# Causal mask: from TensorE matmuls to the VectorE instruction that finds the row maximum

## The chip, the cores and the metric

One core of a Trainium2 chip runs the whole program in one launch. The metric is the device time of the program in microseconds, the median of several runs. Five engines matter: TensorE (matmuls and transposes, results in PSUM), VectorE and ScalarE (element work, both can read and write PSUM), GpSimd (element work in SBUF) and the SP queue, which issues the DMAs. In the profile they are PE (PEld is its weight load), DVE, ACT, POOL and SP. [...]

## The reference

Causal attention with an additive bias over 4 batches, 8 heads, 576 tokens and a head dimension of 64, then two feed-forward blocks over the 2304 tokens:

```python
scores = scale * np.matmul(q, k.transpose(0, 1, 3, 2))
causal = np.triu(np.ones((S, S), dtype=bool), k=1)
cum = np.cumsum(np.maximum(s, 0.0), axis=-1)
bias = -(cum[:, :, :, None] - cum[:, :, None, :])
scores = np.where(causal, -1000000000.0, scores + np.minimum(bias, 0.0))
scores = scores - np.max(scores, axis=-1, keepdims=True)
attn = np.exp(scores)
attn = attn / (np.sum(attn, axis=-1, keepdims=True) + 1e-09)
out = np.matmul(attn, v)

x = out.transpose(0, 2, 1, 3).reshape(B * S, H * D)     # 2304 x 512
x = ((x @ w_a) * (x @ w_b)) @ w_out                     # 512 -> 1536 -> 512
r = np.maximum(x @ w_in, 0.0)                           # 512 -> 2048
out = (r * r) @ w_out2
```

The change concerns the line with `np.where` and the one with `np.max`.

## The kernel before, in words

Three kinds of work follow one another and overlap. Attention works head by head, 32 heads in all. A head's 576 queries are five row blocks (`kb`, L383): one of 64 rows and four of 128. The scores of a head fill four PSUM banks (`banks`, L462): blocks 1 and 2 with 192 and 320 keys, blocks 0 and 3 with 64 and 448 keys, then block 4 in two halves of 288 keys each. A row block needs only the keys up to its last row, so just the piece that holds its last m columns, the diagonal piece, has anything to mask: five of the six pieces of a head.

`softmax` (L555) fills a bank with score matmuls (`st`), whose bias comes in through two extra rows of the operands. The first batch uses one float32 matmul a piece, the later ones two matmuls of split operands (`T` and `t2k`, `t2q`). Before the change the mask is added by TensorE as well: for each diagonal piece one more matmul accumulates `mask` times `identb`, a 128 x 128 bfloat16 tile of -1e9 above the diagonal times an identity (L587 to L592). VectorE then takes each piece's row maximum, negated, into `neg` (L608). Block 4 has two halves, so the smaller of two such values is taken once more (L615). ScalarE writes exp(score + neg) to `e` and the row sums to `sum` (L621). VectorE turns the sums into reciprocals `one`, and VectorE, ScalarE or GpSimd scales `e` by them (L632 to L643). `weigh` (L646) transposes the weights on TensorE into PSUM (`pt`), copies them to SBUF (`ph`, and a low part `pl` in later batches) and multiplies them with the values (`av`).

The first feed-forward block (`moe1`, L834) uses its own matmuls (`ab`, `py`) in chunks of up to 512 tokens, and its weights are decoded on VectorE, ScalarE and GpSimd (`roomxh`, `roomxl`, `words`) while attention runs. The second block (`ph` of hidden units, `po`) comes last.

The order of all this isn't the order of the code. Every operation is given to a planner (`Plan.order`, L145) with a cost in nanoseconds for each engine that may do it, and the planner plays the program through: on each engine the ready operation of the best rank starts next, and some copies and scalings go to whichever engine is free first. On TensorE attention ranks ahead of the feed-forward block, so that `ab` and `py` matmuls fill the places where attention has to wait. The plan fixes each engine's order. The first batch has nothing to fill it with, since the feed-forward block needs its result. In the plan a mask matmul costs 56 (L592) and a row maximum 150 + 1.04 n (L325). Every instruction of the program is issued from L246, so the profile's rows differ by tile names and not by lines. `st`, `neg`, `e`, `one`, `pt`, `ph`, `pl`, `av`, `u`, `vl` belong to attention.

## Time and profile before

| | |
|---|---|
| median of 3 runs | 1128.77 us (1125.85 to 1129.11) |
| span of the profiled execution | 1128.5 us |
| instructions | 15440 |
| TensorE busy over the span | 97% |
| VectorE busy | 55% |
| ScalarE busy | 43% |
| GpSimd busy | 28% |

The profiled execution is one of its own; its span lies 0.3 us under the median. Busy shares over the whole span mix three stages, so the rows below are taken by stretches. [...] What a matmul costs is read from the starts: how much later the next one begins. [...]

### The profile page before, as it was taken

Reading aid. Unit: us, or ns where it says so; the run is one execution under the profiler, and the core shown is the slowest. Engines: PE = TensorE matmul, PEld = TensorE weight load, DVE = VectorE, ACT = ScalarE, POOL = GpSimd, SP = SyncE. Lnnn points to the kernel's source line nnn. Section 1 sums busy time; section 2 is a strip of 40 time slices with the busy share of each in tenths; the row PEclk is TensorE's granted clock in tenths of the full one; section 3 lists DMA queues with packets and bytes.
Section 4 is the critical chain, followed back from the end, with each engine's and each line's share of the span. In section 5 each row is a group of like instructions: output and inputs, shape, how many; then the busy total and the mean of one; then the engine's idle time right before and its main releaser. Section 6 shows DMA issues by size and latency. Waiting matters only on the chain.

```text
span 1128.5 us, 15440 instructions
## 1 busy us (share of the span) xinstructions
PE 1099.6 (97%) x5488; PEld 928.5 (82%) x5488; DVE 625.6 (55%) x1174; ACT 482.9 (43%) x1121; POOL 318.4 (28%) x274
## 2 busy tenths in 40 slices
PE   5998999999999999999999999999999999999998
PEld 3665777778899999899999999888888888888887
DVE  5776797878777777723222358987232232232232
ACT  4545686667666665421121244445232222232222
POOL 2434655655433333200100147766010010000000
PEclk9977899999999999999999999999999999999999
DMA  6433467666544443443433677642110010010010
GB/s 206 153 110 105 142 194 229 187 207 194 151 148 130 135 143 103 143 147 116 164 108 116 186 246 234 195 147 75 38 38 1 21 54 1 1 57 1 1 38 19
DMA packets 83692, 132.10 MB, mean 117 GB/s; under 512 B 9104, under 2 KB 53648, under 8 KB 83616
## 3 DMA queue, kind: packets, MB, share of 16 engines
q1 hardware_dynamic: 83616, 131.12, 37.1%
q8 instruction: 43, 0.70, 0.3%
q14 instruction: 33, 0.27, 0.1%
HBM read 99.54 MB, written 22.69 MB: 108 GB/s over the span
## 4 chain that ended last, share of the span: by engine, by line
PE 90%; DVE 6%; DMA 2%; issue 1%; SPq 0%; ACT 0%; POOL 0%; DVEq 0%; ACTq 0%; POOLq 0%
PE ab L246 24%; PE ph L246 17%; PE po L246 17%; PE py L246 12%; PE av L246 7%; PE st L246 7%; PE pt L246 5%; DVE e L246 1%; DMA roomxh<-in_moe_w_a 1%; SPq L246 0%; DVE neg L246 0%; DMA v_0r<-in_moe_w_in 0%; DVE v_1t L246 0%; DMA v_1r<-in_moe_w_out 0%; DVE v_0t L246 0%
## 5 line engine op out<-in xcount | busy, mean ns | idle before, releaser
L246 DVE SCALAR_TENSOR_TENSOR ph<-ph,r 128x512 f32<-128x512 f32 (+1 forms) x80 | 51.6, 645 | 195.0 <-ACT r L246 195.0
L246 ACT ACTIVATE r<-ph 128x512 f32<-128x512 f32 (+1 forms) x80 | 44.5, 556 | 212.5 <-PE ph L246 212.5
L246 PE MATMUL po<-w2h,g2h 128*128 128x512 f32 x288 | 112.4, 390 | 0.0
L246 PE MATMUL po<-w2h,g2l 128*128 128x512 f32 x288 | 112.3, 390 | 0.0
L246 PE MATMUL po<-w2l,g2h 128*128 128x512 f32 x288 | 112.3, 390 | 0.0
L246 ACT ACTIVATE e<-st,neg 128x192 f32<-128x192 f32 (+2 forms) x192 | 91.1, 479 | 46.8 <-DVE neg L246 42.9
L246 PE MATMUL ab<-xh,wh 128*128 128x448 f32 x288 | 106.3, 369 | 0.0
L246 PE MATMUL ab<-xh,lo 128*128 128x448 f32 x288 | 105.3, 365 | 0.0
L246 PE MATMUL ab<-xl,wh 128*128 128x448 f32 x288 | 105.2, 365 | 0.0
L246 DVE TENSOR_TENSOR ab<-ab,a 128x448 f32<-128x448 f32 (+1 forms) x60 | 38.6, 644 | 105.1 <-PE ab L246 102.5
L246 PE MATMUL pt<-ident,e 128*128 128x128 f32 (+2 forms) x480 | 86.0, 290 | 10.9 <-DVE e L246 9.0
L246 DVE TENSOR_REDUCE neg<-st 128x1 f32<-128x192 f32 (+2 forms) x192 | 77.6, 425 | 27.9 <-PE st L246 19.8
L246 PE MATMUL py<-gh,wh 128*128 128x448 f32 (+1 forms) x240 | 90.8, 379 | 0.5 <-DVE gl L246 0.5
L246 PE MATMUL py<-gh,loo 128*128 128x448 f32 (+1 forms) x240 | 89.0, 371 | 0.0
L246 PE MATMUL py<-gl,wh 128*128 128x448 f32 (+1 forms) x240 | 88.9, 370 | 0.0
L246 PEld LDWEIGHTS pt<-ident,e 128*128 128x128 f32 (+2 forms) x480 | 55.7, 138 | 37.2 <-issue 11.7
L246 PE MATMUL av<-ph,val 128*128 128x256 f32 (+3 forms) x256 | 81.5, 409 | 3.1 <-DVE ph L246 1.4
L246 DVE TENSOR_TENSOR g2l<-ph,g2h 128x512 fp32r<-128x512 f32 (+1 forms) x80 | 51.0, 637 | 41.8 <-ACT g2h L246 37.2
L246 ACT COPY a<-ab 128x448 f32<-128x448 f32 (+1 forms) x60 | 32.6, 544 | 91.6 <-PE ab L246 91.5
L246 PE MATMUL ph<-yhy,w2h 128*128 128x512 f32 (+1 forms) x192 | 67.9, 354 | 0.4 <-DVE gl L246 0.4
L246 PE MATMUL ph<-yhy,w2l 128*128 128x512 f32 (+1 forms) x192 | 67.9, 354 | 0.0
L246 PE MATMUL ph<-yly,w2h 128*128 128x512 f32 (+1 forms) x192 | 67.9, 354 | 0.0
(205 smaller groups left out, 2640.2 us busy)
## 6 DMA issues: line engine op xcount, KB each, us to landing
lo<-wlab SPq DMA_DIRECT2D x48, 512.0 KB
loo<-wlo SPq DMA_DIRECT2D x40, 384.0 KB
v_0r<-in_moe_w_in SPq DMA_DIRECT2D x16, 512.0 KB
v_1r<-in_moe_w_out SPq DMA_DIRECT2D x16, 512.0 KB
roomxh<-in_moe_w_a SPq DMA_DIRECT2D x10, 512.0 KB
roomxh<-in_moe_w_b SPq DMA_DIRECT2D x10, 512.0 KB
roomxl<-in_moe_w_out SPq DMA_DIRECT2D x9, 512.0 KB
out<-o SPq DMA_DIRECT2D x18, 256.0 KB
```

The source lines that it names most:

```text
L246: getattr(eng, method)(*map(real, args), **{k: real(a) for k, a in kw.items()})
```

## The change

The mask becomes one 128 x 448 bfloat16 tile: 320 columns of zero, then the 128 x 128 triangle, now laid out by rows of queries. The mask matmuls and the identity in bfloat16 go. For a diagonal piece the row maximum is taken by `tensor_tensor_reduce`: it adds the last `kn` columns that end at the block's edge of the mask tile, scales by -1, writes the negated masked scores back to the same place in PSUM and keeps the row's minimum in `neg`. The exponential of such a piece then reads negated scores and undoes that by its scale of -1. The one piece without a diagonal (block 4, keys 0 to 287) keeps its reduction. In the planner's eyes the new instruction costs as much as the old one, and the 56 for each mask are gone. The tile in which the mask is made borrows another buffer, and the scratch space of the DMA descriptors is made smaller.

```diff
--- before.py
+++ after.py
@@ -425,16 +425,15 @@
         "affine_select", 128, ident, ident, pattern=[[1, P]], base=0, channel_multiplier=-1,
         compare_op=ALU.not_equal, fill=1.0,
     )
-    identb = const([P, P], BF16, "identb")
-    act("copy", 128, identb, ident)
-    maskf = at([P, 320], F32, "vl", 1, "maskf")[:, :P]
-    gps("memset", 128, maskf, 0.0)
+    MW = 320 + P
+    maskf = at([P, S], F32, "e2", 2, "maskf")[:, :MW]
+    gps("memset", MW, maskf, 0.0)
     gps(
-        "affine_select", 128, maskf, maskf, pattern=[[1, P]], base=0, channel_multiplier=-1,
+        "affine_select", P, maskf[:, 320:], maskf[:, 320:], pattern=[[-1, P]], base=0, channel_multiplier=1,
         compare_op=ALU.is_ge, fill=NEG,
     )
-    mask = const([P, P], BF16, "mask")
-    act("copy", 128, mask, maskf)
+    mask = const([P, MW], BF16, "mask")
+    act("copy", MW, mask, maskf)
 
     spos = at([P, S], F32, "raw", 2, "spos")[: B * H]
     dve("tensor_scalar_max", S, spos, ssb, 0.0)
@@ -567,7 +566,7 @@
                 wide_e = max(kb[blk][0] + kb[blk][1] for blk, _, _ in pieces) > 512
                 e = at([P, S if wide_e else 512], F32, *(("e2", 2) if wide_e else ("e1", 3)), f"e{nm}_{i}")
             off = 0
-            calls, masks, cost, got = [], [], 0, []
+            calls, cost, got = [], 0, []
             for blk, k0, kn in pieces:
                 at_, m = kb[blk]
                 qc = slice(at_, at_ + m)
@@ -582,30 +581,30 @@
                     t1, t2q, t2k, _ = head
                     both = ((t1[:66, 0, qc], t1[:66, 1, ks]), (t2q[:, qc], t2k[:, ks]))
                     cost += 2 * (max(kn, 256) / 2.4 + 13)
-                mine = [("matmul", (to, *ab), {}) for ab in both]
+                mine = [("matmul", (to, *ab), {"stop": True}) for ab in both]
                 calls = mine + calls if kn > 256 else calls + mine
-                if diag:
-                    d0 = off + at_ - k0
-                    masks.append(
-                        ("matmul", (ps[:m, d0 : d0 + m], mask[:, :m], identb[:, :m]), {})
-                    )
-                    cost += 56
                 if k0 == 0:
                     place[blk] = (e, off)
-                got.append((blk, k0, m, to, kn, e[:m, place[blk][1] + k0 : place[blk][1] + k0 + kn]))
+                got.append((blk, k0, m, to, kn, diag, e[:m, place[blk][1] + k0 : place[blk][1] + k0 + kn]))
                 off += kn
             if b == 0:
                 ins = [tq.part("x"), tq.part("c"), tk.part("x"), tk.part("c")]
             else:
                 ins = [t1, t2q, t2k]
-            calls += masks
 
             for z, (_, _, kw) in enumerate(calls):
-                kw.update(start=z == 0, stop=z == len(calls) - 1)
-            pe(cost, calls, ps, [*ins, mask, identb])
-            for blk, k0, m, to, kn, _ in got:
+                kw.update(start=z == 0, skip_group_check=z > 0)
+            pe(cost, calls, ps, ins)
+            for blk, k0, m, to, kn, diag, _ in got:
                 c = blk if k0 == 0 else nq
-                dve("tensor_reduce", kn, out=neg[:m, c : c + 1].part(c), in_=to, op=ALU.max, axis=AX.X, negate=True)
+                if not diag:
+                    dve("tensor_reduce", kn, out=neg[:m, c : c + 1].part(c), in_=to, op=ALU.max, axis=AX.X, negate=True)
+                    continue
+                edge = 320 + m
+                dve(
+                    "tensor_tensor_reduce", kn, out=to, in0=to, in1=mask[:m, edge - kn : edge], op0=ALU.add,
+                    op1=ALU.min, scale=-1.0, scalar=3.0e38, accum_out=neg[:m, c : c + 1].part(c),
+                )
             held += got
             if i + 1 < len(banks) and banks[i + 1][0][1]:
                 continue
@@ -615,11 +614,11 @@
                     op=ALU.min, axis=AX.X, reads=[neg.part(nq - 1), neg.part(nq)],
                 )
             halves = bool(pieces[0][1])
-            for blk, k0, m, to, kn, ee in held:
+            for blk, k0, m, to, kn, diag, ee in held:
                 c = blk if k0 == 0 else nq
                 n_ = nq + 1 if halves else blk
                 act(
-                    "activation", kn + 360, ee.part((blk, k0)), to, AF.Exp, bias=neg[:m, n_ : n_ + 1].part(n_),
+                    "activation", kn + 360, ee.part((blk, k0)), to, AF.Exp, bias=neg[:m, n_ : n_ + 1].part(n_), scale=-1.0 if diag else 1.0,
                     accum_out=tot[:m, blk, int(c == nq) : int(c == nq) + 1].part(c), psum=True,
                 )
             held = []
@@ -1064,7 +1063,7 @@
     import concourse.bacc as bacc
     from concourse.bass_utils import run_bass_kernel_spmd
 
-    nc = bacc.Bacc("TRN2", target_bir_lowering=False, num_devices=1)
+    nc = bacc.Bacc("TRN2", target_bir_lowering=False, num_devices=1, dynamic_dma_scratch_size=1024)
     arrays, args = {}, []
     for name in _INS:
         a = inputs[name]
```

One VectorE call becomes two instructions in the program: the main one and one that writes the accumulated value to `neg`. In the order of instructions both are named ISA.

VectorE at the very first banks of the program, before: the row maxima of the first head's first two banks (`st_0_0_0`, `st_0_0_1`) come one behind the other, and only the first of a bank waits for TensorE.

```order
L246 TENSOR_REDUCE neg_110<-st_0_0_0_135 128x1 [waits PE_49,Pool_49]
L246 TENSOR_REDUCE neg_110<-st_0_0_0_135 128x1
L246 TENSOR_REDUCE neg_110<-st_0_0_1_156 64x1 [waits PE_49]
L246 TENSOR_REDUCE neg_110<-st_0_0_1_156 128x1
L246 TENSOR_REDUCE neg_118<-st_0_1_0_169 128x1 [waits PE_49,Pool_49]
```

The same place now:

```order
L246 ISA st_0_0_0_124,neg_115<-st_0_0_0_124,mask 128x192 [waits PE_49,Pool_49]
L246 ISA neg_115 128x1
L246 ISA st_0_0_0_124,neg_115<-st_0_0_0_124,mask 128x320 [waits DVE_49]
L246 ISA neg_115 128x1
L246 ISA st_0_0_1_141,neg_115<-st_0_0_1_141,mask 64x64 [waits PE_49]
L246 ISA neg_115 64x1
L246 ISA st_0_0_1_141,neg_115<-st_0_0_1_141,mask 128x448 [waits DVE_49]
L246 ISA neg_115 128x1
```

Four instructions have become eight, and the second main one of a bank waits for VectorE itself, since it writes the same bank as the first.

TensorE at the second bank of the last head (`st_3_1_1`, blocks 0 and 3), before: two mask matmuls with their weight loads stand between the scores and the next work.

```order
L246 MATMUL st_3_1_1_5067<-T_1037 128x448
L246 MATMUL st_3_1_1_5067<-t2k_3_1_4866,t2q_3_1_4864 128x448
L246 MATMUL st_3_1_1_5067<-T_1037 64x64
L246 MATMUL st_3_1_1_5067<-t2k_3_1_4866,t2q_3_1_4864 64x64
L246 LDWEIGHTS mask
L246 MATMUL st_3_1_1_5067<-identb,mask 64x64
L246 LDWEIGHTS mask
L246 MATMUL st_3_1_1_5067<-identb,mask 128x128
L246 MATMUL av_2_1_320_5044<-ph_2_1_320_1_5029,vs_2_1_4760 128x128
```

The same place now:

```order
L246 MATMUL st_3_1_1_5085<-T_912 128x448
L246 MATMUL st_3_1_1_5085<-t2k_3_1_4839,t2q_3_1_4859 128x448
L246 MATMUL st_3_1_1_5085<-T_912 64x64
L246 MATMUL st_3_1_1_5085<-t2k_3_1_4839,t2q_3_1_4859 64x64
L246 MATMUL ab_2_1_5097<-xh_4765,wh_1_747 128x448
L246 MATMUL ab_2_1_5097<-xl_4668,wh_1_747 128x448
```

The masks are gone, a score matmul of 64 columns stands last, and the plan has moved: a filling `ab` comes behind the bank instead of an `av`, and it belongs to another chunk and another block of weights. Counted over the whole order, 708 `ab` and 324 `py` matmuls stand ahead of the last `av` now, and 672 and 288 stood there before.

## Rows read from the trace of the kernel before

**Rows 1.** By stretches: us; busy us (count) per engine, clock, DMA share, GB/s.

```profile
8.00:113.00 105.00, 93.11 (x371) 60.30 (x372) 73.14 (x167) 54.02 (x157) 39.14 (x32) 0.85 0.46 145
...
141.00:282.00 141.00, 139.76 (x741) 111.21 (x740) 121.40 (x238) 102.41 (x255) 81.89 (x61) 1.00 0.65 202
282.00:480.00 198.00, 196.99 (x1203) 177.62 (x1203) 149.57 (x341) 119.90 (x322) 65.69 (x58) 1.00 0.45 136
```

**Rows 2.** Tile `mask`: count, ns min/median/max, first and last start in us.

```profile
L246 PE MATMUL st<-identb,mask x160: 194/229/330, 9.7 to 459.6; 128*128 128x128 bf16 x128, 128*64 128x64 bf16 x32
```

**Rows 3.** Waits of TensorE, 113 to 480 us: total us, times, longest.

```profile
PE st L246 <- ACT e L246: 2.0, 2, 1.7
...
PE pt L246 <- DVE pl L246: 0.3, 1, 0.3
```

**Rows 4.** Waits of TensorE, 8 to 113 us.

```profile
PE pt L246 <- DVE e L246: 9.0, 4, 4.0
PE st L246 <- DMA fk<-cum: 7.8, 1, 7.8
```

**Rows 5.** Chain of waits, 8 to 141 us, shares by engine and tile.

```profile
by line: PE st L246 29.1%; PE av L246 26.5%; PE pt L246 16.3%; PE ab L246 7.7%; DVE e L246 7.6%; DVE neg L246 1.8%; DVE roomxl L246 1.8%; DVE u L246 1.7%; issue 1.7%; DVE ph L246 1.3%; DVE raw_1q L246 0.9%; DVE T L246 0.8%; ACT e L246 0.7%;
```

**Rows 6.** Timeline of TensorE, 410 to 440 us: start, us, operation.

```profile
412.23 0.38 PE L246 MATMUL st<-identb,mask 128*64 128x64 bf16 x2
412.41 0.45 PE L246 MATMUL ab<-xh,wh 128*128 128x448 f32 x1
412.70 0.37 PE L246 MATMUL ab<-xl,wh 128*128 128x448 f32 x1
412.91 0.37 PE L246 MATMUL ab<-xh,lo 128*128 128x448 f32 x1
...
419.47 0.28 PE L246 MATMUL av<-ph,vs 128*128 128x256 f32 x1
419.59 0.28 PE L246 MATMUL av<-pl,vs 128*128 128x256 f32 x1
...
419.98 0.23 PE L246 MATMUL st<-identb,mask 128*128 128x128 bf16 x1
420.02 0.36 PE L246 MATMUL av<-ph,vs 128*128 128x256 f32 x1
420.22 0.28 PE L246 MATMUL av<-pl,vs 128*128 128x256 f32 x1
...
424.86 0.29 PE L246 MATMUL st<-identb,mask 128*128 128x128 bf16 x2
424.95 0.45 PE L246 MATMUL st<-T 66*128 66x448 f32 x1
425.24 0.36 PE L246 MATMUL st<-t2k,t2q 128*128 128x448 f32 x1
```

**Rows 7.** Timeline of all engines, 0 to 20 us.

```profile
9.66 0.42 PE L246 MATMUL st<-identb,mask 128*128 128x128 bf16 x2
...
9.88 2.22 PE L246 MATMUL st<-fk,fq 65*128 65x448 f32 x4
```

**Rows 8.** VectorE groups by shape, whole span: busy us, mean ns, idle before.

```profile
L246 DVE TENSOR_TENSOR ab<-ab,a 128x448 f32<-128x448 f32 x48 | 30.3, 631 | 99.3 <-PE ab L246 96.8 <-ACT w2h L246 2.3
...
L246 DVE TENSOR_REDUCE neg<-st 128x1 f32<-128x448 f32 x32 | 19.5, 608 | 1.2 <-ACT e L246 1.2
...
L246 DVE TENSOR_TENSOR_SCAN cum<-spos 32x576 f32<-32x576 f32 x1 | 1.3, 1346 | 0.0
```

**Rows 9.** Timeline of VectorE, 40 to 46 us and 418 to 425 us.

```profile
44.12 0.14 DVE L246 TENSOR_REDUCE neg<-neg 128x1 f32<-128x2 f32 x1
44.19 0.61 DVE L246 TENSOR_REDUCE neg<-st 128x1 f32<-128x448 f32 x1
...
421.46 0.46 DVE L246 TENSOR_REDUCE neg<-st 128x1 f32<-128x288 f32 x1
421.96 0.15 DVE L246 TENSOR_REDUCE neg<-neg 128x1 f32<-128x2 f32 x1
```

## The prediction

> **What bounds the kernel now.** I read the table by stages first. [...] From 141 to 480 us the other batches run with matmuls of the first MoE between them: TensorE is busy 139.76 of 141 and 196.99 of 198 us at full clock, VectorE 121.40 and 149.57 [rows 1]. Behind 480 us there is no attention left (the last mask starts at 459.6, [rows 2]). The list of waits says what the filled stretch lacks: in all of 113 to 480 us TensorE waited eight kinds of time, from 2.0 us down to 0.3, 4.5 us together [rows 3]. So there a matmul that goes away is time that comes back, unless something else turns late. The first batch is another thing: its longest wait is for normalised scores (`pt` for VectorE's `e`), 9.0 us in 4 waits [rows 4], and the chain of waits from 8 to 141 us is 79.6% TensorE (29.1 st, 26.5 av, 16.3 pt, 7.7 ab) and, by its named pieces, 15.9% VectorE [rows 5]. A gain on TensorE counts there for four fifths, a loss on VectorE for a fifth or more.

> **What is removed.** Five mask matmuls a head (row blocks 0 to 4 have one diagonal piece each), 32 heads: 160 matmuls and 160 weight loads. Their listed duration must not be multiplied: a median of 229 ns in the same row would give 36.6 us, but matmuls overlap, and what one costs is how far it puts off the start of the next. Near 420 us a bank with one mask: the mask starts at 419.98, the next matmul 0.04 us later, and that one takes until 420.22, 0.20 us, where the same `av` without a mask ahead takes 0.12 (419.47 to 419.59). So 0.04 of its own and 0.08 that the next pays, because its weights could not load under so short a matmul: 0.12 us. The pair behind the 64-row block: 412.23 to 412.41, 0.18 us, and the next `ab` starts its successor after 0.29 us where 0.21 is usual (412.70 to 412.91): 0.18 to 0.26. The pair of the bank with 192 and 320 columns: 424.86 to 424.95, 0.09, and the following 448 columns take 0.29, 0.08 over the usual: 0.09 to 0.17 [rows 6]. The lower ends hold if the score matmul that now comes last exposes the next load just as the mask did. Together 0.31 to 0.55 us a head (0.04 to 0.12 for the single one). I take 0.44, near the upper middle, since behind 192 or 288 score columns more of the load is covered than behind a mask. From 113 us on there are 24 heads: 24 x 0.44 = 10.6 us (7.4 to 13.2).

> In the first batch a pair costs 0.22 us (9.66 to 9.88) [rows 7], one alone by that 0.11: 2 x 0.22 + 0.11 = 0.55 a head, 4.4 us for 8 heads. With 79.6% of the chain on TensorE that is 3.5 us.

> **What is added.** Each of these five row maxima becomes two VectorE instructions: one that adds the mask, writes the negated scores back to PSUM and takes the minimum, and one that writes the accumulated minimum to `neg`. No row of before has either, so I bound them. The main one reads PSUM and SBUF and writes PSUM, as `ab<-ab,a` does: 631 ns at 448 columns, where the reduction has 608. That is 23 ns more [rows 8]. For the second one the nearest row is the reduction of two columns: the next instruction starts 0.07 us after it (44.12 to 44.19) [rows 9]. So 0.02 + 0.08 = 0.10 us a mask. In the two banks with a pair the second sum now waits for the first, since both write the same bank; before, the two reductions followed each other unheld. What such a wait on its own engine costs is in a row pair: the small reduction that needs the result of the one ahead starts at 421.96, 0.04 us behind that one's end (421.46 + 0.46), where 44.19 lies 0.07 us ahead of the end of 44.12 + 0.14 [rows 9]. That is 0.11 us, twice a head. Together 5 x 0.10 + 2 x 0.11, some 0.75 us a head. Below: nothing, if the new form streams like the old one, its read is covered and other work stands between the two of a pair; I don't count on less, because an instruction is added. Above: the only VectorE row that carries a value from element to element is the cumulative sum, 1346 ns for 576 elements [rows 8]. A reduction of 576, scaled from the 608 ns of 448, would take 782 at most. The scan has 564 ns more, 0.98 an element, and a head has 64+192+320+448+288 = 1312 such elements: 1.3 us, with five reads and two waits 1.9 us a head. I take 0.75, as the `ab<-ab,a` row shares every operand's place with the new instruction and the scan does not.

> [...]

> Who hides 0.75 us a head? From 141 to 282 us VectorE has 141 - 121.40 = 19.6 us idle, from 282 to 480 us 48.4 [rows 1]. A head in the filled stretch takes some (480-113)/24 = 15.3 us. In the first part that leaves 2.1 us a head, in the second 3.7. Averages hide lateness, though: these engines run in order, and behind a late row maximum stand the exponentials on ScalarE, then the transposes `pt` on TensorE, with filling matmuls queued behind them. For that latency the change takes and gives: a bank's scores are ready earlier by its masks, and its maxima later by 0.10 us (one mask) to 0.31 (a pair). Lateness may cost between nothing and all the 24 x 0.75 = 18 us. I take a quarter, 4.5 us, because with all that was late there before TensorE lost just 4.5 us [rows 3].

> In the first batch 8 x 0.75 = 6.0 us are added to VectorE, which is busy 73.14 of 105 us. If all its work stood on the chain in equal part, 15.9% of it where the engine is busy for 70%, a quarter would count, 1.4 us; all of it would be 6.0. I take 2.0, a third, because the maxima stand on that chain more often than the decoding of weights does.

> Costed at nothing: the wider mask (a 448-column memset on GpSimd and one ScalarE cast, instead of two casts of 128) is made in the first microseconds, while TensorE waits 7.8 us for its first operands [rows 4]; the first masks started at 9.66 [rows 7]. If that cover failed, a fraction of a microsecond would show. The exponential's scale of -1 is a constant of an instruction that is there already. The smaller DMA scratch issues nothing. The moved order: VectorE gets three more operations of the kinds that may go to either engine, and the plan puts 708 `ab` and 324 `py` matmuls ahead of the last attention matmul, against 672 and 288. All of them have to run anyway, so at a full TensorE their place costs nothing. Behind 480 us the work is the same.

> **The sum**, against the profiled span of 1128.5 us: -10.6 + 4.5 for the filled stretch, -3.5 + 2.0 for the first batch: -7.6, 1120.9. The median of the runs, 1128.77, lies 0.3 above the span, so 1121. What a measurement of this kernel can tell from no change is about 0.3%, 3.4 us.

> **Rivals.**
> Larger gain: masks at their full 0.55 us (13.2 us), no new lateness, and the first batch's 3.5 with 1.4 lost: -15.3, 1113. For it: eight small waits only [rows 3]. Against it: a short score matmul of 64 columns now stands where the pair stood, and something must load under it.

> Gain eaten (no change): TensorE's place is given back as waits. The 10.6 us are met by 24 x 0.44 of new waits, if the fillers that the plan lays behind each head are just enough for a maximum that comes in time. Or the first batch spends more of its time at the lower clock: its 0.30 of 105 us are 31.5 us [rows 1], and half as much again would cost some 8 us at half speed. Longer waits of TensorE like the 9.0 us for `e` [rows 4] could bring that about, which one trace cannot show. Either leaves 1125 to 1131, say 1128. For it: the first batch's clock and VectorE's 86% in 141 to 282 us. Against: latency per bank hardly changes.

> Slower: the new instruction streams like the scan. Then a head has 1.9 us more on VectorE, 17 us for the nine heads of 141 to 282 us against 19.6 idle. Barely no bound by work, but a bank with a pair, 512 columns, has its maxima 0.50 + 0.16 + 0.11 us later and its scores 0.1 to 0.2 earlier, and the third bank some 0.3 later: 1.5 us a head. With half of it in the open, 24 x 0.75 = 18 us. The first batch would lose half of 8 x 1.9, 7.6 us, on its chain. -10.6 + 18 - 3.5 + 7.6 = +11.5, 1140. It decides from where half of a head's lateness is more than the 0.44 us gained: about 0.9 us a head that no room takes up. For it: a form that this trace does not show. Against: `ab<-ab,a`.

> That the change does not do what it says is excluded: the order has no row with the mask on TensorE any more.

> **How the numbers follow.** Forecast 1121: 0.55. Larger gain: 0.15. Gain eaten: 0.17. Slower: 0.13. The range leaves a tenth at either end: low 1110, below the larger gain since a stretch of lower clock may also go away; high 1133, which takes in the eaten gain and little of the slower case. The forecast's own range is 1114 to 1126: the mask cost's bounds are 3 us to either side, the two shares of lateness as much again. Faster by over 0.3%: the first two, 0.70. Within 0.3%: most of the third, 0.15. Slower: the fourth and an end of the third, 0.15.

> **What would show it.** In the profile after: no matmul with a mask; the main instruction within 30 ns of the reduction at each width, and its accumulator read some 0.07 to 0.1 us from start to start; VectorE busy about 16 us longer (160 x 0.10); the stretch up to the last attention matmul ends about as late as before, but with more `ab` and `py` matmuls done; TensorE's waits from 113 us to the end of attention under 10 us in all; the stretch without attention shorter by about what was gained. The prediction is wrong in its VectorE term if the read shows 0.2 us or more between starts, or the main one grows faster than 1 ns an element. It is wrong in its TensorE term if starts around a diagonal bank lie no closer than before. If the first batch ends more than 3 us off from where the sum puts it, 1.5 us earlier than now, it was the clock or the chain of that batch that decided.

## The result, and the profile after

The changed kernel takes 1112.03 us, the median of 4 runs (1109.73 to 1115.63), against 1127.31 us for the kernel before, measured beside it (1120.12 to 1129.11). The ratio is 0.9877, with a 95% interval from 0.9836 to 0.9917: 13.9 us less, between 9.4 and 18.5. The forecast had the sign and the range right, but gave 7.6 us, below that interval. The time lies 2 us above the low end of the range and outside the forecast's own 1114 to 1126: it is where the rival "larger gain" stood (1113). The profiled executions differ by 16.1 us of span (1128.5 and 1112.4).

Where the time went is read by the same stretches as [rows 1]. The columns are busy time and count of TensorE, its weight loads, VectorE, ScalarE and GpSimd, then the granted clock, the DMA share and GB/s.

```profile
8.00:113.00 105.00, 91.62 (x373) 61.06 (x374) 80.55 (x237) 63.89 (x184) 42.78 (x33) 0.92 0.51 158
113.00:141.00 28.00, 28.00 (x137) 22.11 (x136) 24.14 (x49) 20.47 (x51) 18.10 (x14) 0.95 0.57 173
141.00:282.00 141.00, 134.56 (x672) 106.64 (x671) 121.92 (x266) 91.72 (x230) 81.27 (x62) 0.98 0.63 192
282.00:480.00 198.00, 197.60 (x1182) 180.90 (x1182) 155.57 (x405) 120.67 (x324) 57.33 (x51) 1.00 0.46 141
```

Two things stand out. The first stretch has a clock of 0.92 where it had 0.85. And TensorE idles 6.4 us between 141 and 282 us, where it idled 1.2, yet the whole is faster. The start of the feed-forward block behind the first batch, the first `ab` matmul on TensorE's timeline, tells how much was gained by then. The columns are start, duration and operation. Before:

```profile
124.06 1.20 PE L246 MATMUL ab<-x,wh 128*128 128x512 f32 x2
```

After:

```profile
111.95 0.95 PE L246 MATMUL ab<-x,wh 128*128 128x512 f32 x2
```

It comes 12.1 us earlier, although the first batch was to gain 1.5. By the prediction's own test that is the clock or the chain of that batch. The last attention matmul starts at 483.3 us, 2.5 earlier than the 485.8 of before, and the order has 72 more `ab` and `py` matmuls ahead of it. The other 13.6 us of the 16.1 are gained behind it, where those 72 no longer stand: 0.19 us each, where an `ab` of 448 columns takes 0.21 from start to start.

On VectorE, the groups by shape that answer to [rows 8] (busy us, mean ns of one, idle before):

The new instruction takes 630 ns where the reduction took 608. The read is listed at 134 ns, but VectorE's timeline of the first microseconds shows what it costs:

```profile
10.20 0.37 DVE L246 CUSTOM_DVE_ANT_0 st<-st,mask 128x192 f32<-128x192 f32 x1 [3.01 <-PE st L246]
10.48 0.14 DVE L246 DVE_READ_ACCUMULATOR2_ANT neg<- 128x1 f32 x1
10.66 0.50 DVE L246 CUSTOM_DVE_ANT_0 st<-st,mask 128x320 f32<-128x320 f32 x1
...
20.25 0.46 DVE L246 CUSTOM_DVE_ANT_0 st<-st,mask 128x288 f32<-128x288 f32 x1
20.63 0.14 DVE L246 DVE_READ_ACCUMULATOR2_ANT neg<- 128x1 f32 x1
20.63 0.68 DVE L246 SCALAR_TENSOR_TENSOR roomxl<-roomxh,roomxl 128x512 int32<-128x512 int32 x1
```

(The new instruction is called the sum here and below.) At 20.63 the next instruction starts with the read, not behind it, 0.38 us after the sum. Before, a bare reduction of this width put off the next by 0.37:

```profile
20.98 0.46 DVE L246 TENSOR_REDUCE neg<-st 128x1 f32<-128x288 f32 x1 [0.55 <-PE st L246]
21.35 0.42 DVE L246 TENSOR_SCALAR roomxl<-roomxh 128x512 int32<-128x512 int32 x1
```

In a pair, the second sum starts 0.18 us behind the read, since it waits for the first. The small reduction of block 4, which needs what the read wrote, is held as well:

```profile
420.11 0.46 DVE L246 CUSTOM_DVE_ANT_0 st<-st,mask 128x288 f32<-128x288 f32 x1
420.48 0.14 DVE L246 DVE_READ_ACCUMULATOR2_ANT neg<- 128x1 f32 x1
420.65 0.16 DVE L246 TENSOR_REDUCE neg<-neg 128x1 f32<-128x2 f32 x1
```

It starts 0.54 us behind the sum, and in [rows 9] it started 0.50 behind the bare reduction. So the read is nearly free for an instruction that does not need its value, and the one that does waits 0.17 us for it.

On TensorE, the banks that answer to [rows 6]:

```profile
410.35 0.39 PE L246 MATMUL st<-T 66*128 66x448 f32 x1
410.58 0.37 PE L246 MATMUL st<-t2k,t2q 128*128 128x448 f32 x1
...
410.82 0.22 PE L246 MATMUL st<-t2k,t2q 128*64 128x64 f32 x1
410.88 0.45 PE L246 MATMUL ab<-xh,wh 128*128 128x448 f32 x1
411.17 0.36 PE L246 MATMUL ab<-xl,wh 128*128 128x448 f32 x1
...
414.41 0.30 PE L246 MATMUL st<-t2k,t2q 128*128 128x288 f32 x1
414.54 0.37 PE L246 MATMUL ab<-xh,wh 128*128 128x448 f32 x1
414.75 0.37 PE L246 MATMUL ab<-xl,wh 128*128 128x448 f32 x1
```

Behind the score matmul of 64 columns, the `ab` still takes 0.29 us until the next start, as it did behind the masks: the 0.08 that the prediction put down to the next weight load stays (that load is listed from 410.85 for 0.19 us, and the matmul of 64 columns starts at 410.82), and only the pair's own 0.18 us is gone. The first two lines stand behind a score matmul of 192 columns, where the other pair was: the 448 columns take 0.23 and not 0.29, so 0.15 of that pair's 0.17 is gone. Behind 288 columns the `ab` takes the usual 0.21, so the single mask's 0.12 is gone whole.

TensorE's waits from 113 to 480 us, which answer to [rows 3], and two from 8 to 113 us, to [rows 4] (total us, times, longest):

```profile
PE st L246 <- ACT e L246: 3.1, 3, 1.5
PE pt L246 <- DVE ph L246: 1.8, 2, 1.4
PE av L246 <- DVE ph L246: 0.8, 2, 0.4
PE pt L246 <- DVE e L246: 0.6, 2, 0.4
PE pt L246 <- DVE pl L246: 0.3, 1, 0.3
```

```profile
PE st L246 <- DMA fk<-cum: 8.0, 1, 8.0
PE pt L246 <- DVE e L246: 6.8, 4, 3.4
```

In the filled stretch that is 6.6 us against 4.5. The waits for `e` in the first batch are shorter, 6.8 against 9.0.

The chain of waits from 8 to 141 us, to [rows 5]:

```profile
by line: PE av L246 24.2%; PE st L246 22.5%; PE pt L246 13.0%; PE ab L246 9.5%; DVE e L246 4.9%; issue 4.9%; DVE roomxl L246 3.7%; DVE st L246 2.6%; DMA fq<-in_q 2.1%; DVE wt L246 2.0%; DVE u L246 1.4%; DVE roomxh L246 1.2%; DVE x L246 1.2%
```

TensorE's share fell from 79.6% to 69.2%, and the new sums stand on it as `DVE st`, with 2.6% of 133 us, 3.5 us.

Of [rows 2] nothing is left on TensorE. The tile `mask` is now read by VectorE alone, from 10.2 to 461.1 us:

```profile
L246 DVE CUSTOM_DVE_ANT_0 st<-st,mask x160: 199/455/657, 10.2 to 461.1; 128x192 f32<-128x192 f32 x32, 128x320 f32<-128x320 f32 x32, 64x64 f32<-64x64 f32 x32, 128x448 f32<-128x448 f32 x32
```

### The profile page after: what moved, and what is told of

Read it like the earlier page. It is cut to its first block, busy times and chain, and to the rows that moved or that the text cites. A ratio compares the mean times of both kernels' runs of the same rounds, so it can differ in the third digit from the quotient of the medians.

```text
span 1112.4 us, 15234 instructions
## 1 busy us (share of the span) xinstructions
PE 1078.8 (97%) x5328; PEld 914.4 (82%) x5328; DVE 639.8 (58%) x1337; ACT 481.2 (43%) x1123; POOL 312.7 (28%) x268
## 4 chain that ended last, share of the span: by engine, by line
PE 78%; DVE 11%; DMA 4%; issue 3%; ACT 1%; POOL 1%; SPq 1%; DVEq 0%; POOLq 0%; ACTq 0%
PE ab L246 21%; PE po L246 17%; PE ph L246 16%; PE py L246 10%; PE av L246 5%; PE st L246 5%; PE pt L246 4%; DVE roomxl L246 2%; DVE e L246 1%; DVE st L246 1%; DMA v_1r<-in_moe_w_out 1%; SPq L246 1%; DMA raw_3q<-in_q 1%; DMA raw_2q<-in_q 1%; DVE ab L246 1%
## 5 line engine op out<-in xcount | busy, mean ns | idle before, releaser
L246 PE MATMUL pt<-ident,e 128*128 128x128 f32 (+2 forms) x480 | 84.9, 287 | 12.1 <-DVE e L246 7.5
L246 DVE CUSTOM_DVE_ANT_0 st<-st,mask 64x64 f32<-64x64 f32 (+4 forms) x160 | 68.2, 434 | 15.1 <-PE st L246 9.8
L246 ACT CAST gh<-ab 128x448 fp32r<-128x448 f32 (+1 forms) x60 | 32.6, 543 | 87.7 <-DVE ab L246 87.6
L246 ACT CAST g2h<-ph 128x512 fp32r<-128x512 f32 (+1 forms) x80 | 43.5, 544 | 57.1 <-DVE ph L246 57.0
```

What stands on the lines that cost most here:

```text
L246: getattr(eng, method)(*map(real, args), **{k: real(a) for k, a in kw.items()})
```

## How the runs are compared: the clock of every run

Each run comes with its mean granted clock. Over 72 of the 73 runs of the kernel before that were made beside the experiments (of two with the same time and clock one is counted) it is not one value. 41 runs stand at 0.986 and take 1126.6 us on average, 11 at 0.983 with 1130.4, 15 at 0.992 with 1121.8. The clock records of both profiles, before and after, have two levels, 0.50 and 1.00. Before, the first `av` pair of 256 columns after 83 us takes 0.96 us from its start to that of the next operation (83.43 to 84.39, clock 0.50), and one at 43.78 takes 0.49 (to 44.27, clock 1.00). Span times (1 - clock) times 2 is the time spent at 0.50, if the rest is at 1.00: some 38, 31 and 18 us. So the same program varies by 9 us with its time at the lower clock. Within the kernels of this case, over 188 runs, a microsecond more at the lower clock costs 0.46 us, close to the half that levels of 0.50 and 1.00 give.

So each run's time can be carried to full clock by taking off span times (1 - clock). The table's last columns do this. Their intervals are 95%. One of e2's twelve runs took 3714.88 us at a clock of 1.00: it counts in e2's median (1120.46 without it) and in no other column. With 0.46 in place of one half, the differences move by at most 0.4 us, and by 0.8 in the last two rows.

| kernel | ratio to before | median us | us at a clock of 0.50, mean | at full clock, against before |
|---|---|---|---|---|
| before | 1 | 1125.5 to 1126.9 | 29.0 | 1111.4 |
| e1: masks dropped, old order | 0.9925 [0.9894, 0.9957] | 1116.58 | 28.7 | -8.6 ± 1.3 |
| e2: whole change, old order | 0.9952 [0.9931, 0.9973] | 1121.31 | 33.4 | -6.6 ± 0.7 |
| the change (with e3) | 0.9877, 0.986 | 1112.03, 1110.18 | 22.7 | -11.3 ± 1.1 |
| e4: before, another order | 0.9998 [0.9976, 1.002] | 1126.08 | 23.6 | +2.8 ± 1.1 |
| e5: old work, new order | 0.9968 [0.9949, 0.9988] | 1122.19 | 23.2 | -0.2 ± 1.0 |
| e6: change, order of old costs | 0.9966 [0.9938, 0.9993] | 1122.94 | 29.9 | -4.7 ± 1.1 |
| e7: change, sums into `e` | 0.9982 [0.9956, 1.0007] | 1122.79 | 33.8 | -5.6 ± 0.5 |
| e8: no wait in pairs | 0.9878 [0.9848, 0.9909] | 1111.73 | 24.1 | -11.1 ± 1.1 |
| e9: change from batch 1 on | 0.9914 [0.988, 0.9947] | 1115.58 | 27.9 | -9.3 ± 1.0 |
| e10: plan knows the read | 0.9914 [0.9888, 0.994] | 1114.68 | 26.2 | -8.3 ± 1.3 |
| e11: before, kept busy | 0.9937 [0.9914, 0.996] | 1119.67 | 13.4 | +0.8 ± 0.8 |
| e12: change, kept busy | 0.9835 [0.9805, 0.9865] | 1106.52 | 12.2 | -10.1 ± 0.8 |

The first step is to read the change itself this way: 11.3 us at full clock, and 6.3 us less at the lower clock, worth 3.1. Together 14.4 us.

## Experiments: the work apart from the order

The theories were three. By the first (M), the new work is worth all of it, so the masks cost more than was reckoned and lateness less. By the second (O), the order that came with the change has a part of its own. By the third (C), it is the clock of the first batch.

**e1: the mask matmuls dropped, the order of before kept.** It leaves the causal mask out altogether. The plan keeps its cost of 56 a mask, so nothing moves.

```diff
-            calls += masks
 
             for z, (_, _, kw) in enumerate(calls):
-                kw.update(start=z == 0, stop=z == len(calls) - 1)
+                kw.update(start=z == 0, stop=True, skip_group_check=z > 0)
```

> Leaves the causal mask out: no mask matmul and no mask in the row maximum; every engine keeps the instruction order of before. Theory M (the mask matmuls' own TensorE time is the gain): 12 to 16 us faster than before, of it about 10 us behind the first batch and 3 to 5 in it. Theory O (most of the gain is the new order that the plan found): 3 to 6 us faster. Theory C (the clock of the first batch): the stretch up to the first filling ab matmul is 10 us or more shorter and its granted clock rises from 0.85 to over 0.90.

Measured: 0.9925, 8.6 us at full clock. With no VectorE work added at all, the old order still gives only this, where 10.6 + 3.5 = 14.1 us of masks were reckoned. In plain time it is some 8.5 us, between what the first two theories asked for. The clock of the first batch does not explain it, since the time at the lower clock stays as it was (28.7 and 29.0 us).

**e2: the whole change in the order of before.** The planner plays through the old operations. What they issue is exchanged behind its back.

```diff
+    def emit(eng, *calls):
+        op = pl.ops[-1]
+        op.ways = {eng: (op.ways[eng][0], list(calls), op.ways[eng][2])}
...
                 dve("tensor_reduce", kn, out=neg[:m, c : c + 1].part(c), in_=to, op=ALU.max, axis=AX.X, negate=True)
+                if diag:
+                    edge = 320 + m
+                    emit("DVE", ("tensor_tensor_reduce", (), dict(
+                        out=to, in0=to, in1=mask[:m, edge - kn : edge], op0=ALU.add, op1=ALU.min, scale=-1.0,
+                        scalar=3.0e38, accum_out=neg[:m, c : c + 1].part(c),
+                    )))
```

> The whole change, result as the reference, but each engine keeps the order of before (the accumulator reads come on top). Theory M: what e1 gains less 5 to 8 us for VectorE's added work, so 6 to 10 us faster than before, and VectorE's extra shows as waits of TensorE. Theory O: within 3 us of before, and the changed kernel stands 10 us ahead of it. If VectorE's added work costs nothing: as e1, within 2 us.

Measured: 0.9952, 5.4 us less in plain time, again between the two theories, and 6.6 us at full clock. VectorE's new work gives back some 2.0 ± 1.4 us of e1's gain. The work alone does not bring the measured gain, so the first theory falls.

**e3: the changed kernel once more**, on the same chip as e1 and e2, with no edit.

> The changed kernel as it is, to stand on the same chip as the others. All theories: 10 to 18 us faster than before, ratio 0.984 to 0.992.

Measured: 0.986 [0.9824, 0.9896], 1110.18 us. The interval lies clear of e2's. In plain time the same work in two orders differs by over half of the gain, at full clock by 4.7 of 11.3 us.

**e5: the old work in the new order.** The changed program's plan, but plain reductions and mask matmuls are issued.

```diff
+                if diag:
+                    d0 = off + at_ - k0
+                    masks.append(
+                        ("matmul", (ps[:m, d0 : d0 + m], mask[:, 320 : 320 + m], identb[:, :m]), {"stop": True})
+                    )
...
+            calls += masks
...
+                emit("DVE", ("tensor_reduce", (), dict(out=neg[:m, c : c + 1].part(c), in_=to, op=ALU.max, axis=AX.X, negate=True)))
```

> The work of before (mask matmuls on TensorE, plain row maxima), result as the reference, in the instruction order of the changed kernel on every engine. Theory O (the order is worth 10 us whatever the mask is made of): 8 to 12 us faster than before, ratio 0.990 to 0.993. Theory S (the new order pays only because the masks are gone): within 4 us of before. Where the gain is, by theory O: the first batch up to the first filling ab matmul is 5 us or more shorter than in the profile of before, with a granted clock above 0.88.

Measured: 0.9968. The first batch does end earlier, as theory O had it: the first `ab` starts at 115.04 us, 9.0 earlier than before, at a clock of 0.93 from 8 to 113 us. But the gain is not 8 to 12 us. At full clock nothing is left of it (-0.2 ± 1.0): in these runs the order alone only shortens the lower clock, from 29.0 to 23.2 us. The four corners at full clock are thus 0, -6.6 (work), -0.2 (order) and -11.3 (both). Some 4.5 us belong to neither alone. (The smaller DMA scratch is in e2 and e5 both, so a cost of its own would be a part of these 4.5 us. No run tells it apart.)

Where they are shows in the stretches. TensorE's idle time from 141 to 480 us is the length less the busy time. e2:

```profile
141.00:282.00 141.00, 135.20 (x697) 107.97 (x697) 121.74 (x277) 100.58 (x251) 81.78 (x61) 1.00 0.65 200
282.00:480.00 198.00, 195.32 (x1163) 177.41 (x1163) 152.08 (x404) 119.27 (x320) 62.67 (x57) 1.00 0.45 140
```

e5:

```profile
141.00:282.00 141.00, 137.31 (x697) 109.07 (x697) 115.92 (x221) 91.58 (x229) 81.61 (x62) 0.96 0.65 193
282.00:480.00 198.00, 196.81 (x1200) 178.41 (x1198) 152.27 (x342) 119.45 (x324) 58.96 (x52) 1.00 0.46 138
```

In the old order the new work takes the idle time from 2.2 us [rows 1] to 8.5: of what the masks set free, 6.3 us become waits. (e1, with no VectorE work added at all, already idles 7.3 us.) That the plan laid too few `ab` and `py` behind each head is a reading of this, and no run shows it by itself. In the new order, the old work idles 4.9 us and the new work 6.8 (5.4 in e3's profile), so 0.5 to 1.9 us more. The difference is 4.4 to 5.8 us, as much as the corners leave over. These are single profiles. e5's first row also shows that the lower clock is not the first batch's alone: 0.96 over 141 us are some 11 us at a clock of 0.50, and the change's 0.98 some 6, where before had 1.00.

**e9: the new order, the first batch with mask matmuls and plain reductions.**

```diff
+                if diag and b == 0:
+                    d0 = off + at_ - k0
+                    masks.append(
+                        ("matmul", (ps[:m, d0 : d0 + m], identb[:, :m], mask[:, 320 : 320 + m]), {"stop": True})
+                    )
...
+                if b == 0:
+                    emit("DVE", ("tensor_reduce", (), dict(out=neg[:m, c : c + 1].part(c), in_=to, op=ALU.max, axis=AX.X, negate=True)))
```

> The changed kernel in its own order, result as the reference, but the first batch does its masks on TensorE and plain row maxima as before; the other three batches have the change. If the new work pays in the filled stretch (24 heads): ratio to before 0.987 to 0.990, within 3 us of the changed kernel. If it pays in the first batch: 0.993 or more, at least 6 us behind the changed kernel. By the prediction's own terms (1.5 us in the first batch, 6 behind it) 1 to 3 us behind the changed kernel.

Measured: 0.9914, in plain time 3.6 and 5.4 us behind the change's two medians, which is neither of the first two expectations. From e5 to e9 the 24 later heads get the new work: 9.1 us at full clock. (The plain ratios say 6.1, but e9's runs happened to spend 27.9 us at the lower clock and e5's 23.2, in a first batch with the same matmuls by number, shape and order.) From e9 to the change the first batch follows: 2.0 ± 1.3 us at full clock.

## Experiments: other orders, and the suspected costs

**e4: the kernel before, planned without the masks' cost.** Only the order moves.

```diff
-                    cost += 56
```

> The kernel before with its mask matmuls, but the planner counts them as 0 and not 56, so that only the order moves. Theory M: within 4 us of before. Theory O: 5 us or more away from before, to either side, since an order alone then moves the time as much as the change did.

Measured: 0.9998, in plain time as theory M had it. But it spends less time at the lower clock (23.6 us) and is 2.8 us slower at full clock. A plan that leaves the masks out of its costs is no gift to a kernel that has them.

**e6: the changed kernel, planned with the masks' cost.**

```diff
+                cost += 56 * diag
```

> The changed kernel, result as the reference, but the planner still counts 56 for each mask that is gone, so that only the order moves. Theory O in its plain form (any order will do as well as another, the gain comes from the masks): as the changed kernel within 3 us. If the order is luck: anywhere from 2 to 12 us slower than the changed kernel.

Measured: 0.9966, 4.7 us at full clock, and 11 to 13 us behind the change, as "the order is luck" had it. The change under a plan made for the old work gains about as little as e2.

**e10: the plan is told of the second instruction**, 180 columns' worth, 187 ns.

```diff
-                    "tensor_tensor_reduce", kn, out=to, in0=to, ...
+                    "tensor_tensor_reduce", kn + 180, out=to, in0=to, ...
```

> The changed kernel, result as the reference, with the new instruction planned at 187 ns more (about what a pair was measured to cost on VectorE), so that only the order moves. If a plan nearer to the truth is a better one: 2 to 6 us faster than the changed kernel. If orders are luck: anywhere between the changed kernel and 12 us behind it, as the orders of e6 and e7 were.

Measured: 0.9914, 8.3 us at full clock. The price given to the plan is far over the read's real cost, and the order that results is a worse one.

**e7: the masked scores go to `e` in SBUF**, where the exponential reads them, so that the second sum of a pair need not wait. The order moves with it.

```diff
-                    "tensor_tensor_reduce", kn, out=to, in0=to, ...
+                    "tensor_tensor_reduce", kn, out=ee.part((blk, k0)), in0=to, ...
...
-                    ... ee.part((blk, k0)), to, AF.Exp, ...
+                    ... ee.part((blk, k0)), ee.part((blk, k0)) if diag else to, AF.Exp, ...
```

> The changed kernel, result as the reference, but the masked scores go to the tile e in SBUF and the exponential reads them there. No main instruction waits for the one ahead of it on VectorE, and a score bank is free once VectorE is through; the order moves too. If the pair's wait and the held banks matter: 2 to 5 us faster than the changed kernel. If not: within 3 us, or slower by the longer exponentials from SBUF (160 x 0.04 us on ScalarE).

Measured: 0.9982, over 10 us behind the change, which neither expectation had. It settles nothing on the wait, because both the order and the lower clock (33.8 us) got worse.

**e8: the wait in the pairs taken away, in the new order.** The sums go to four scratch tiles in turn, and the exponential reads the scores as they are.

```diff
+    unused = [const([P, MW], BF16, f"unused{i}") for i in range(4)]
...
+                emit("DVE", ("tensor_tensor_reduce", (), dict(
+                    out=unused[turn[0] % 4][:m, :kn], in0=to, ...
```

> The changed kernel in its own order, but the masked scores go to scratch tiles that take turns and the exponential reads the unmasked ones: the mask stays out of the exponential. 53 of 60 waits of VectorE for itself go. If such a wait costs 0.1 to 0.2 us and reaches the end: 2 to 5 us faster than the changed kernel. If it is hidden: within 2 us.

Measured: 0.9878, at full clock the same as the change (-11.1 and -11.3), with 53 of 60 such waits gone. The 0.18 us of a pair are hidden.

## Experiments: the clock

**e11: the kernel before, with 32 useless matmuls** of the identity with itself, 8 ahead of the first transposes of each pair's first head in the first batch. The order is that of before. **e12: the same in the changed kernel.**

```diff
             pe(len(calls) * 107, calls, ps, ins)
+            if b == 0 and h == 0 and g0 == 0 and i == 0:
+                idle = [("matmul", (ps[:, :P], ident, ident), {"start": True, "stop": True}) for _ in range(8)]
+                op = pl.ops[-1]
+                op.ways = {"PE": (op.ways["PE"][0], [*idle, *op.ways["PE"][1]], False)}
```

> The kernel before in its own order, result as the reference, with 8 matmuls of no use (128 columns, float32, identity by identity) put ahead of the first transposes of four heads of the first batch, where TensorE waits: 32 matmuls, about 7 us of TensorE at full clock. If the lower clock of the first batch follows from these waits and costs time: its granted clock from 8 to 113 us rises from 0.85 to 0.90 or more, and the kernel is 2 to 6 us faster in spite of the added work. If the clock has another cause: clock as before, and 0 to 6 us slower.

> The same 32 matmuls of no use in the changed kernel, result as the reference. If the lower clock that is left there (0.92) comes from waits at these four places: 1 to 4 us faster than the changed kernel. If its waits lie elsewhere (for operands of the scores): as the changed kernel or up to 6 us slower.

Measured: e11 0.9937, so work was added and the program became 7.1 us faster, a little more than expected, at a clock of 0.95 from 8 to 113 us. The time at the lower clock fell from 29.0 to 13.4 us, worth 7.8, and at full clock the additions cost 0.8. The place is seen between 70 and 90 us, in stretches of 5 us. Before:

```profile
70.00:75.00 5.00, 3.82 (x18) 2.66 (x17) 4.72 (x6) 2.28 (x5) 4.70 (x5) 0.85 0.65 198
75.00:80.00 5.00, 5.00 (x14) 2.42 (x13) 3.09 (x10) 1.77 (x7) 1.20 (x1) 0.50 0.80 261
80.00:85.00 5.00, 5.00 (x17) 3.90 (x16) 2.20 (x7) 2.60 (x11) 0.10 (x1) 0.50 0.02 7
85.00:90.00 5.00, 5.00 (x15) 2.59 (x14) 1.65 (x5) 2.56 (x5) 2.18 (x4) 0.50 0.00 0
```

TensorE waits 1.18 us, and this is its timeline there:

```profile
73.73 1.06 PE L246 MATMUL pt<-ident,e 128*64 128x128 f32 x4 [1.18 <-DVE e L246]
74.58 1.70 PE L246 MATMUL st<-fk,fq 65*128 65x448 f32 x2
```

Then come 15 us at a clock of 0.50, in which a full TensorE gets 44 matmuls done (two of them stand in two rows). e11, the same stretches, and the useless matmuls (`pt<-ident`) on its timeline:

```profile
70.00:75.00 5.00, 5.00 (x31) 3.41 (x30) 4.53 (x11) 2.75 (x9) 2.38 (x2) 1.00 0.75 214
75.00:80.00 5.00, 5.00 (x29) 3.36 (x28) 3.99 (x12) 4.26 (x12) 2.09 (x3) 1.00 0.27 111
80.00:85.00 5.00, 4.71 (x24) 3.01 (x25) 4.29 (x10) 2.15 (x9) 1.61 (x2) 1.00 0.28 105
85.00:90.00 5.00, 4.57 (x29) 3.60 (x27) 4.61 (x13) 4.09 (x12) 3.46 (x3) 1.00 0.06 15
```

```profile
68.14 2.00 PE L246 MATMUL pt<-ident 128*128 128x128 f32 x16
```

They stand where TensorE waited, and the clock stays at 1.00. The first `ab` then starts at 112.31 us, 11.8 earlier than in the kernel before, with no work removed.

```profile
112.31 1.20 PE L246 MATMUL ab<-x,wh 128*128 128x512 f32 x2
```

e12 gives 0.9835, with a median of 1106.52 us the fastest of all. Its interval overlaps e3's, but all its runs lie at a clock of 0.992 to 0.997, those of the change at 0.986 to 0.992. At full clock the added matmuls cost it about 1 us.

## Why the prediction was right, and where it was wrong

**The mask's price held.** The pair of [rows 6] gave back 0.18 us, the single mask 0.12 and the other pair 0.15: 0.45 a head, where 0.44 was taken.

**VectorE's term was over-reckoned, and mattered little.** The main instruction cost +22 ns (23 were reckoned). The read cost about 0.01 us and not 0.08, where the next instruction does not need it: 0.38 us from start to start with it, 0.37 without. The pair's wait cost 0.18 us and not 0.11, and e8 shows it hidden. VectorE is busy 14.2 us longer (639.8 against 625.6; 16 were forecast). (Attention runs on to 485.8 us in the kernel before, past the 480 that the prediction names. That does not move the forecast.)

**The filled stretch**: -6.1 was forecast (-10.6 masks, +4.5 lateness), and e5 to e9 gave -9.1 at full clock. With the masks at 10.6, lateness was 1.5. In the old order, where TensorE idles 6.3 us more, the 4.5 was rather too small. So what lateness costs depends on the order that the new work meets.

**The first batch**: -1.5 was forecast, and e9 to the change gave -2.0 ± 1.3 at full clock. That term was right. The 12.1 us by which its end moved are mostly clock and order: e11 moves it by 11.8 with no gain in work, and e5, with the old work, by 9.0.

**The step that failed** is "All of them have to run anyway, so at a full TensorE their place costs nothing." It failed twice. In the order that the plan makes once the masks are out of its costs the new work leaves TensorE fewer waits, and 6.6 us of gain become 11.3 (e2 against the change). And TensorE is not at full clock all the way: the new order spends 23.2 us at the lower level where the old one spent 29.0 (e5), worth 2.9 ± 1.5 us. Together that is 4.7 + 2.9 = 7.6 us. In the old order the work gave 1.0 us less than the forecast. That leaves 6.6, close to the 6.8 by which the forecast fell short of 14.4.

The forecast's base had a share as well in the time that it gave, 1121 (1128.77 was taken, and 1127.31 measured beside the change). The profiled execution of before, at 0.85 in its first batch, ran 1128.5 us of span, as the eleven runs at 0.983 do. The typical run of that kernel is at 0.986. The rival "gain eaten" took the lower clock's share of the first batch, 0.30 of 105 us, from the 0.85 of [rows 1] (0.15 is lost, at half speed), and counted it as a risk on one side alone, and only the low end of the range allowed for the other. It went the other way. That the time came out where "larger gain" stood is luck: that rival counted masks at 0.55 us a head and no new lateness, and the masks gave 0.45 while TensorE idled longer.

What ties the orders together is TensorE's idle time over the whole span (span less its busy time), 28.9 us before. It is longer by 6.1 us in e1, 7.4 in e2, 9.5 in e6, 9.2 in e7, 5.0 in e10, 5.3 in e8, and 4.7 and 3.4 in the two profiles of the change. Add that to each one's gain at full clock, and the masks come to between 13.3 and 16.4 us in every order, where 14.1 were reckoned. So the forecast of 6.5 us for lateness was near what the old order showed in size, and too much for the new one. But 6.1 of the old order's 7.4 come without any new VectorE work (e1): they are waits as "gain eaten" described them, and not late maxima. These are single profiles beside means of runs, and agree no better than these 3 us.

What stays open: why the planner's order leaves the new work fewer waits than those of e6, e7 and e10. And whether the new order's shorter time at the lower clock is more than luck: e9, in the same order, has 27.9 us, and e6 and e10, with the same work, have 29.9 and 26.2.

## What to carry to other kernels

Where a planner sets the order, a change has two effects, its work and its new order: run each without the other before believing either, because here, at full clock, the work alone was worth 6.6 us, the order alone nothing, and both together 11.3. Read each run's granted clock before comparing times of a few tenths of a per cent, and carry them to one clock. Where TensorE waits in a stretch without fillers, price the clock that it loses there, not only the wait: here 32 matmuls in such places cost 0.8 us at full clock and took 15.6 us off the time at 0.50 (e11).

## What the runs showed of the hardware that was not expected

Useless matmuls paid. A wait of 1.18 us ahead of transposes stood before 15 us at a clock of 0.50, and 32 matmuls in such places took 15.6 us off the time at that level (e11) and 10.5 us in the changed kernel (e12).

The time of one unchanged program went in steps with its clock: 0.983, 0.986 and 0.992, with 1130.4, 1126.6 and 1121.8 us.

A VectorE instruction that only writes an accumulated value is listed at 134 ns, and a next one that does not need the value starts at the same time (20.63). One that needs it starts 0.17 us later (420.48 to 420.65).
